# A two-stage strided convolution with a joint layer: first samples loaded in even and odd parts, taps issued by ScalarE, a leading tile of 396 columns

## The chip, the cores and the metric

The kernel runs on one core of a Trainium2 chip. The metric is the device time of one execution in microseconds, the median of several. The kernel before took 253.08 us, the median of three runs from 252.41 to 253.65.

The core's engines are named as in the profile: PE is TensorE (matrix products and transposes into PSUM), DVE is VectorE, ACT is ScalarE, POOL is GpSimd and SP is SyncE, which issues transfers here. Each engine works through its own list in order, and engines wait for each other by semaphores.

## The reference

Shapes: x is (2, 4000, 512), w1 and w2 are (5, 512, 512), g is (2, 8, 512), and w_f, w_g, w_o are (512, 512), all in bf16.

```python
xp = jnp.pad(x, ((0,0),(2,2),(0,0)))
h = sum over i of einsum("btc,cd->btd", xp[:, i:i+T, :], w1[i])
h = gelu(h)[:, ::2, :]                     # 2000 steps a sample
f = the same with w2 on h, gelu, [:, ::2]  # 1000 steps a sample
fe = f @ w_f ;  ge = g @ w_g
j = tanh(fe[:, :, None, :] + ge[:, None, :, :])
out = j @ w_o                              # (2, 1000, 8, 512)
```

So there are two convolutions of five taps, each with stride two, and then a joint layer over 16 pairs of sample and g row.

## The kernel before

Channels lie on the partitions, in four blocks of 128 (`NK`), and time steps are the columns of the matrix products. An output step t of the first convolution reads inputs 2t-2 to 2t+2.

The first convolution is done in two ways. A leading direct tile of the first sample makes `2 * NA` = 432 outputs, the plain way: five taps by four output blocks `m` by four input blocks `k`, 80 products of 432 columns (`direct`, lines 683 to 689), accumulated in PSUM banks 0 to 3. The taps go in the order 0, 4, 2, 1, 3. Taps 0, 4 and 2 read only even input steps, taps 1 and 3 only odd ones (`tap_at`, line 672). The rest goes through `Triple` (lines 554 to 596), which makes three outputs of a polyphase row together from nine products instead of fifteen. Its rows are sums and differences of six input phases (`z`, from xq or xp) that ACT and DVE make (`step`), and its weights are sums of taps that DVE and ACT make (`w1part`, lines 534 to 550: `ssum`, `w1_x` and `w1_t`). The first two triples are tiles of `N3` = 262 columns of the first sample, from `xq[0]` and `xq[1]`. Two triples for the second sample come from `xp[2]` and `xp[0]`, then two with w2 for the second convolution. Each triple is worked in four units, one for an output block, whose steps `s1` to `s5` interleave (lines 814 to 824).

The samples of the direct tile come as rows: `load_xr` (lines 445 to 449) puts four successive steps on one partition, 128 partitions in `xr[0]` and 90 in `xr[1]`. PE turns them with 32 transposes against `ident` (lines 493 to 508): for each of the two buffers, even steps (`pp` = 0), then odd ones. DVE copies the two results of `xr[0]` from PSUM to `xs[0]`, ACT those of `xr[1]`. Ahead of them PE runs eight products on zeros (`warm_mm`). The samples of the triples come by turning loads (`load_x6`, lines 451 to 456): a transfer that transposes, one for each of six phases, 272 columns each.

All loads of the head are issued by SP, in this order: `xr[0]`, `xr[1]`, w1[0] in two halves of its output columns, w1[4], w1[2], w1[1], w1[3], and then the turning loads of `xq[0]` (phases 4, 0, 2, 1, 3, 5), of `xq[1]` and of `xp[2]`. Each whole tap waits until the load three before it has landed (`o.after.append(came[-3].idx)`, line 469).

The order on each engine is planned by `Plan.schedule` (lines 157 to 225). It simulates the engines from the costs given with each operation, and for transfers from one shared wire: 1.8 us after issue a transfer may start, and it takes its bytes at a given rate (320 bytes a ns, 170 for turning loads). On PE, SP and POOL the lowest number among the ready operations goes first; on ACT and DVE the one that is due soonest. Up to `pl.pin = False` (line 694) the order of each engine is as written; from there on the plan sets it. At run time each engine follows the planned order strictly and waits for whatever comes late.

Of the kernel before, what the change touches and what calls it, by code (L numbers as in the profile page):

```python
# [50 lines left out]
class Psum:  # L51
# [6 lines left out]
    def pair(self, lo, step, n):  # L58
        ap = self.h[:, lo:lo + 2 * step].rearrange("p (s c) -> p s c", s=2)[:, :, 0:n]
        cells = np.unique(np.concatenate([np.arange(lo, lo + n), np.arange(lo + step, lo + step + n)]) // 512)  # L60
        return View(ap, cells, True)
# [6 lines left out]
class Plan:  # L68
# [25 lines left out]
    def dma(self, eng, fn, reads=(), writes=(), sem=None, nbytes=524288, rate=320e3):  # L94
# [3 lines left out]
        o.reads, o.writes, o.cost, o.pin, o.after, o.wire = tuple(reads), tuple(writes), 0.43, True, [], nbytes / rate  # L98
# [58 lines left out]
    def schedule(self, pred):  # L157
# [30 lines left out]
        wire, lock, start = 0.0, 0.0, [0.0] * n  # L188
        for _ in range(n):
# [24 lines left out]
            if o.dma:  # L214
                wire = max(wire, t + 1.8) + o.wire
                end = max(wire, t + 2.0)
# [85 lines left out]
def bass_standalone__seq2seq_rnn_t_joint__speech_kernel(  # L302
# [25 lines left out]
    NA, N3 = 216, 262  # L328
# [7 lines left out]
    NWARM = 8  # L336

    with ExitStack() as es:
# [106 lines left out]
        def load_xr(rt):  # L445
            n = NR[rt]
            dst = xr[rt].rows(0, n).map(lambda a: a.rearrange("p r k c -> p (r k c)"))
            src = x[0, 4 * P * rt:4 * (P * rt + n), :].rearrange("(p r) c -> p (r c)", r=4)
            return pl.dma("sp", lambda e: e.dma_start(dst.ap, src), (), (dst,), nbytes=n * 4 * 2 * D)

        def load_x6(buf, b, ph, j0, col, n=336):
# [4 lines left out]
            pl.dma("sp", lambda e: e.dma_start_transpose(out=dst.ap, in_=src), (), (dst,), nbytes=n * 2 * D, rate=170e3)  # L456

        came = [load_xr(rt) for rt in range(2)]
        act(warm[0:1], warm[1:2], ACT.Gelu_apprx_tanh)

        def load_w1(i):
            src = w1[i].rearrange("(k c) d -> c k d", c=P)
            if len(came) == 2:
                h = D // 2
                for sl in (slice(0, h), slice(h, D)):
                    o = pl.dma("sp", lambda e, sl=sl: e.dma_start(w1_sb[i, :, sl].ap, src[:, :, sl]), (), (w1_sb[i, :, sl],), nbytes=262144)
            else:
                o = load_w("sp", w1_sb[i], src)
                o.after.append(came[-3].idx)
            came.append(o)  # L470

        def load_xq(i, ph):
            load_x6(xq[i], 0, ph, 2 * NA // 3 + i * N3 - 2, 0, -(-(N3 + 3 - i) // 16) * 16)

        for kind, i in (('w', 0), ('w', 4), ('w', 2), ('w', 1), ('w', 3), ('x', 4), ('x', 0), ('x', 2), ('x', 1), ('x', 3), ('x', 5)):
            if kind == "w":
                load_w1(i)
            else:
                load_xq(0, i)
        for ph in (4, 0, 2, 1, 3, 5):  # L480
            load_xq(1, ph)
# [8 lines left out]

        warm_mm(NWARM)
        psb = ps.h[:, :].bitcast(BF16)
        for rt in range(2):
            for pp in range(2):
                bk, n = 4 + 2 * pp + rt, NR[rt]
                pv = View(psb[:, bk * 1024:(bk + 1) * 1024].rearrange("p (r k c) -> p r k c", r=2, k=NK)[:, :, :, 0:n], np.array([bk]), True)

                def fn(e, rt=rt, pp=pp, pv=pv, n=n):
                    for r in range(2):
                        for k in range(NK):  # L500
                            ins = e.transpose(pv.ap[:, r, k, :], xr[rt].h[0:n, 2 * r + pp, k, :], ident.h[0:n, 0:n])
                    return ins
# [184 lines left out]
        for i in taps:  # L687
            for m in range(NK):
                direct(i, m)
# [437 lines left out]
```

## Time and profile before

| what | value |
|---|---|
| median of three runs | 253.08 us (252.41 to 253.65) |
| profiled execution: its span | 251.3 us |
| profiled execution: own time beside the span | not listed on the page; the median is 1.8 us above the span |
| PE busy | 245.7 us, 98% |
| DVE, ACT busy | 211.8 us, 210.5 us |
| granted clock | 1.00 |
| first transpose, first product of the direct tile | 4.58 us, 7.47 us |
| first product of the first triple | 22.12 us |
| last landing of xr, w1, xq[0] | 5.86, 14.40, 24.27 us |

How to read it: times in the timeline are microseconds from the start of the span. The landing of a transfer is the last of its 16 semaphore updates in the trace. Products on PE are pipelined, so the listed length of one is longer than the distance to the next; where I give what a product costs, it is that distance. In the table by stage each engine has its busy time and its number of instructions. In the chain of waits each piece is what the next one waited for.

### The profile page before, as it was taken

The page shows a single profiled execution, that of the slowest core. Times are in us where ns is not written, and L with a number is a line of the kernel's source. Part 1 is how long each engine was busy: PE and PEld are TensorE (multiplying, and loading weights), DVE is VectorE, ACT ScalarE, POOL GpSimd, SP SyncE. Part 2 cuts the span into 40 slices and gives each one's busy share as a digit, 9 for nine tenths or more (in the row PEclk, how much of TensorE's full clock was granted, in tenths as well). Part 3 has the DMA queues.
Part 4 walks back from the last instruction along what each step waited for, and adds up shares of the span by engine and source line. Part 5 has one row for each costly group of instructions (what it writes and reads, how often), then busy time and mean ns, then how long its engine had stood idle before and what let it go on. Part 6 is the DMA issues. An engine that isn't in the chain of part 4 may idle for free.

```text
span 251.3 us, 5205 instructions
## 1 busy us (share of the span) xinstructions
PE 245.7 (98%) x1920; PEld 184.6 (73%) x1920; DVE 211.8 (84%) x347; ACT 210.5 (84%) x353; POOL 106.7 (42%) x109
## 2 busy tenths in 40 slices
PE   8999999999999999999999999999999999999994
PEld 4556788877666666666467878777788888778873
DVE  1699999967999997971547798999999999999892
ACT  2388699878959869963799999999999999997763
POOL 1000000000000000003338899698998999699930
PEclk9999999999999999999999999999999999999999
DMA  7999999988400052000002223322344336534648
GB/s 212 326 174 176 186 156 208 176 144 274 148 0 3 0 182 71 1 1 3 0 1 85 83 86 127 127 86 83 127 132 164 128 120 219 187 123 148 207 137 266
DMA packets 57392, 31.92 MB, mean 127 GB/s; under 512 B 33837, under 2 KB 57149, under 8 KB 57367
## 3 DMA queue, kind: packets, MB, share of 16 engines
q1 hardware_dynamic: 57367, 31.59, 48.0%
q8 instruction: 15, 0.25, 0.4%
q14 instruction: 10, 0.08, 0.1%
HBM read 7.71 MB, written 16.38 MB: 96 GB/s over the span
## 4 chain that ended last, share of the span: by engine, by line
PE 85%; DMA 6%; DVE 5%; ACT 2%; SPq 1%; issue 1%; DVEq 0%
PE acc L423 85%; DMA xq<-in_x_dram 3%; DMA w_sb<-in_w_dram 2%; DVE row L410 2%; DMA xr<-in_x_dram 1%; DVE xq L410 1%; SPq L456 1%; ACT sn L843 1%; DVE og L410 0%; ACT jT L415 0%; DVE sn L844 0%; DVE ssum L511 0%; ACT ost L843 0%; DVE w_t L410 0%; DVE w_x L410 0%
## 5 line engine op out<-in xcount | busy, mean ns | idle before, releaser
L410 DVE TENSOR_TENSOR og<-acc,sn 128x512 bf16<-128x512 f32 x87 | 56.9, 681 | 3.9 <-PE acc L423 3.1
L415 ACT ACTIVATE jT<-feT,geT 128x1000 bf16<-128x1000 f32 (+6 forms) x56 | 51.7, 975 | 0.5 <-DVE feT L736 0.4
L423 PE MATMUL acc<-tw,ss 128*128 128x256 f16 x348 | 48.0, 273 | 0.0
L912 POOL TENSOR_TENSOR ss<-jT 128x512 f16<-128x512 bf16 x28 | 33.8, 1219 | 12.9 <-ACT jT L415 10.6
L423 PEld LDWEIGHTS acc<-tw,ss 128*128 128x128 f16 x348 | 33.5, 98 | 7.3 <-DVE sn L844 0.3
L843 ACT ACTIVATE sn<-acc 128x512 f32<-128x512 f32 x52 | 31.5, 620 | 3.5 <-PE acc L423 3.2
L423 PE MATMUL acc<-row,w_sb 128*128 128x334 bf16 (+1 forms) x192 | 33.1, 295 | 0.2 <-DVE row L410 0.2
L423 PE MATMUL acc<-wo_sb,jT 128*128 128x256 bf16 (+1 forms) x196 | 31.7, 288 | 0.0
L407 POOL MEMSET hT<- 128x8 bf16 (+2 forms) x6 | 0.7, 148 | 71.8 <-ACT hT L415 66.8
L423 PE MATMUL acc<-row,w_x 128*128 128x262 bf16 (+1 forms) x192 | 28.2, 290 | 0.0
L415 ACT ACTIVATE jX<-feT,geT 128x1000 bf16<-128x1000 f32 (+4 forms) x28 | 25.0, 932 | 0.0
L423 PEld LDWEIGHTS acc<-row,w_sb 128*128 128x128 bf16 x192 | 18.5, 98 | 6.8 <-DVE row L410 0.5
L423 PEld LDWEIGHTS acc<-wo_sb,jT 128*128 128x128 bf16 x196 | 19.2, 98 | 5.3
L423 PEld LDWEIGHTS acc<-row,w_x 128*128 128x128 bf16 x192 | 18.8, 98 | 5.4
L415 ACT ACTIVATE sd<-acc 128x334 f32<-128x334 f32 (+1 forms) x48 | 20.5, 431 | 1.9 <-PE acc L423 1.3
L912 POOL TENSOR_TENSOR ss<-jX 128x512 f16<-128x512 bf16 x18 | 20.9, 1176 | 1.2 <-ACT jX L415 0.7
L415 ACT ACTIVATE hT<-acc 128x262 bf16<-128x262 f32 (+2 forms) x36 | 15.1, 432 | 6.7 <-PE acc L423 6.6
L511 DVE SCALAR_TENSOR_TENSOR acc<-acc,sd 128x334 f32<-128x334 f32 (+1 forms) x24 | 11.6, 483 | 10.4 <-PE acc L423 10.3
L844 DVE COPY sn<-acc 128x512 f32<-128x512 f32 x25 | 16.9, 682 | 2.4 <-PE acc L423 2.2
L423 PE MATMUL acc<-wo_sb,ss 128*128 128x256 bf16 x116 | 17.9, 273 | 0.0
L423 PE MATMUL acc<-hT,w_sb 128*128 128x334 bf16 x96 | 17.4, 305 | 0.0
L912 POOL TENSOR_TENSOR ss<-ss,jT 128x512 f16<-128x512 f16 x14 | 16.4, 1181 | 0.7 <-PE acc L423 0.4
(105 smaller groups left out, 501.6 us busy)
## 6 DMA issues: line engine op xcount, KB each, us to landing
out_dram<-og SPq DMA_DIRECT2D x44, 256.0 KB, 2.3
w_sb<-in_w_dram SPq DMA_DIRECT2D x9, 512.0 KB, 5.0
out_dram<-og SPq DMA_DIRECT2D x14, 128.0 KB, 2.7
out_dram<-ost SPq DMA_DIRECT2D x7, 128.0 KB, 2.0
xr<-in_x_dram SPq DMA_DIRECT2D x1, 512.0 KB, 3.4
w_sb<-in_w_dram SPq DMA_DIRECT2D x2, 256.0 KB, 5.1
wf_sb<-in_w_f_dram SPq DMA_DIRECT2D x1, 512.0 KB, 3.6
wg_sb<-in_w_g_dram SPq DMA_DIRECT2D x1, 512.0 KB, 4.7
```

The costliest lines, as they stand in the source:

```text
L407: pl.op("pool", lambda e: e.memset(v.ap, 0.0), (), (v,))
L410: pl.op(eng, lambda e: e.tensor_tensor(out=o.ap, in0=a.ap, in1=b.ap, op=op), (a, b), (o,), 0.02 + 2.14e-3 * o.ap.free_size() if eng == "po ...
L415: pl.op("act", lambda e: e.activation(o.ap, i.ap, func, scale=scale, bias=0.0 if bias is None else bias.ap), rd, (o,), o.ap.free_size() * ...
L423: ins = e.matmul(o.ap, lhsT=l.ap, rhs=r.ap, start=start and n == 0, stop=stop and n == len(pairs) - 1, skip_group_check=not check)
L456: pl.dma("sp", lambda e: e.dma_start_transpose(out=dst.ap, in_=src), (), (dst,), nbytes=n * 2 * D, rate=170e3)
L511: pl.op(eng, lambda e: e.scalar_tensor_tensor(out=o.ap, in0=a.ap, scalar=f, in1=b.ap, op0=ALU.mult, op1=add), (a, b), (o,), vec_cost(o, (a ...
L843: pl.flex({"act": (lambda e: e.activation(o.ap, v.ap, ACT.Copy), 0.05 + n * 0.833e-3), "dve": (lambda e: e.tensor_copy(out=o.ap, in_=v.ap) ...
L844: "dve": (lambda e: e.tensor_copy(out=o.ap, in_=v.ap), 0.065 + n * 1.04e-3)}, (v,), (o,))
L912: fn = lambda e, o=S[i], x=x, y=y, op=op: e.tensor_tensor(out=o.ap, in0=x.ap, in1=y.ap, op=op)
```

## The change

The change is confined to the head of the kernel, and to the sizes of the tiles of the first sample.

- `NA` goes from 216 to 198, so the direct tile has 396 columns; `N3` goes from 262 to 268; `xr[1]` has 72 partitions instead of 90.
- `load_xr` loads the even steps or the odd steps of a buffer, in runs of 1 KB. The even parts are issued by SP, the odd ones by ACT.
- The taps of w1 are issued by ACT, with no wait between them: w1[0] in two halves of its input blocks, w1[4], then the table load with the first activation, then the two odd parts of xr, then w1[2], w1[1], w1[3].
- SP issues the turning loads right behind the two even parts.
- PE: six products on zeros, the even transposes of `xr[0]`, two more on zeros, the even transposes of `xr[1]`, then tap 0 and tap 4, then the odd transposes of both, then taps 2, 1 and 3. DVE copies the even parts to `xs[0]`, ACT the odd ones.
- Tap 0 is done in halves: columns 0 to 127 of each group first, which need only `xr[0]`, then the other 70; and within each the input blocks 0 and 1 before 2 and 3.
- The memsets of the borders of `hT` are moved behind the taps.
- The planner has one wire for each issuing engine, 1.6 us from issue to start, other rates (245 for taps, 185 for turning loads, 80 for phases 4 and 0 of `xq[0]`), and the copies of the even parts cost 0.55 ns an element.

```diff
     def pair(self, lo, step, n):
-        ap = self.h[:, lo:lo + 2 * step].rearrange("p (s c) -> p s c", s=2)[:, :, 0:n]
+        lo_ap = self.h[:, lo:lo + n]
+        ap = bass.AP(tensor=lo_ap.tensor, offset=lo_ap.offset, ap=[list(lo_ap.ap[0]), [step, 2], [1, n]])
...
-        wire, lock, start = 0.0, 0.0, [0.0] * n
+        wire, lock, start = {}, 0.0, [0.0] * n
...
-                wire = max(wire, t + 1.8) + o.wire
-                end = max(wire, t + 2.0)
+                wire[e] = max(wire.get(e, 0.0), t + 1.6) + o.wire
+                end = max(wire[e], t + 2.0)
...
-    NA, N3 = 216, 262
+    NA, N3 = 198, 268
...
-    NWARM = 8
+    NWARM = 6
...
-        def load_xr(rt):
+        def load_xr(rt, pp, eng):
             n = NR[rt]
-            dst = xr[rt].rows(0, n).map(lambda a: a.rearrange("p r k c -> p (r k c)"))
-            src = x[0, 4 * P * rt:4 * (P * rt + n), :].rearrange("(p r) c -> p (r c)", r=4)
-            return pl.dma("sp", lambda e: e.dma_start(dst.ap, src), (), (dst,), nbytes=n * 4 * 2 * D)
+            dst = xr[rt].rows(0, n, slice(pp, 4, 2)).map(lambda a: a.rearrange("p r k c -> p r (k c)"))
+            src = x[0, 4 * P * rt:4 * (P * rt + n), :].rearrange("(p r) c -> p r c", r=4)[:, pp::2, :]
+            return pl.dma(eng, lambda e: e.dma_start(dst.ap, src), (), (dst,), nbytes=n * 2 * 2 * D)
...
-            pl.dma("sp", lambda e: e.dma_start_transpose(out=dst.ap, in_=src), (), (dst,), nbytes=n * 2 * D, rate=170e3)
-
-        came = [load_xr(rt) for rt in range(2)]
+            pl.dma("sp", lambda e: e.dma_start_transpose(out=dst.ap, in_=src), (), (dst,), nbytes=n * 2 * D, rate=rate, cost=n * 0.005)
+
+        def load_w1(i, parts=1):
+            n = NK // parts
+            for k in range(0, NK, n):
+                src = w1[i, k * P:(k + n) * P].rearrange("(k c) d -> c k d", c=P)
+                dst = w1_sb[i, k:k + n]
+                pl.dma("act", lambda e, dst=dst, src=src: e.dma_start(dst.ap, src), (), (dst,), nbytes=n * 131072, rate=245e3)
+
+        load_xr(0, 0, "sp")
+        load_w1(0, 2)
+        load_xr(1, 0, "sp")
+        load_w1(4)
         act(warm[0:1], warm[1:2], ACT.Gelu_apprx_tanh)
...
+        for rt in range(2):
+            load_xr(rt, 1, "act")
+        load_w1(2)
+        load_w1(1)
+        load_w1(3)
...
+        for i in range(2):
+            for ph in (4, 0, 2, 1, 3, 5):
+                load_xq(i, ph)
...
         warm_mm(NWARM)
...
+        turn(0, 0, "dve")
+        warm_mm(2)
+        turn(1, 0, "dve")
...
-        def both(i, k):
+        def both(i, k, q0=0, n=NA):
...
-        for i in taps:
+        for q0, n in ((0, P), (P, NA - P)):
+            for ks in ((0, 1), (2, 3)):
+                for m in range(NK):
+                    mm(ps.pair(m * NT + q0, NA, n), [(w1_sb[0, k, m * P:(m + 1) * P], both(0, k, q0, n)) for k in ks],
+                       q0 == 0 and ks[0] == 0, False, False)
+        for i in taps[1:]:
+            if i == 2:
+                turn(0, 1, "act")
+                turn(1, 1, "act")
             for m in range(NK):
                 direct(i, m)
+        for b in range(B):
+            memset(hT[b][4:6, :, HOFF - 1:HOFF])
+            memset(hT[b][:, :, HOFF + NT3:HOFF + NT3 + 2])
```

`turn(rt, pp, eng)` is the old body of the turning loop for one buffer and one parity, with the copy on the engine named.

## The prediction

> **What bounds the kernel now.** I read the page first (span and busy shares), then the table by stage, then the chain of waits, then the timeline of the first 34 us, and last the DMA view of three stretches.
>
> The page, span and the three busiest engines:
>
> ```profile
> span 251.3 us, 5205 instructions
> PE 245.7 (98%) x1920; PEld 184.6 (73%) x1920; DVE 211.8 (84%) x347; ACT 210.5 (84%) x353; POOL 106.7 (42%) x109
> ```
>
> PE is busy for 98% of the span, so time can only come off where PE is idle or where its columns become fewer. The same by stage (busy us of PE, PEld, DVE, ACT, POOL; clock; DMA share; GB/s):
>
> ```profile
> 1.20:7.47 6.27, 5.73 (x41) 3.34 (x41) 1.33 (x2) 1.85 (x4) 0.72 (x8) 1.00 0.97 273
> 7.47:22.12 14.65, 14.65 (x81) 7.84 (x81) 12.72 (x21) 9.95 (x15) 0.00 (x0) 1.00 1.06 226
> 22.12:28.83 6.71, 6.51 (x58) 5.31 (x56) 6.71 (x13) 5.75 (x13) 0.24 (x2) 1.00 1.03 185
> 28.83:60.00 31.17, 31.17 (x270) 26.31 (x271) 27.31 (x48) 26.14 (x51) 0.50 (x3) 1.00 1.02 180
> ```
>
> Up to 7.47 PE only warms up and turns samples; from 7.47 to 22.12 it runs the direct tile without a hole; from 28.83 on it is full again. Between 22.12 and 28.83 it has small holes while DVE is busy for all 6.71 us. So two things decide the head: when the direct tile can start, and whether DVE has the rows ready when it ends. The chain of waits says the second aloud (start, us, what):
>
> ```profile
> 0.74 3.43 DMA xr<-in_x_dram
> 4.19 4.75 DMA w_sb<-in_w_dram
> 11.51 6.42 DMA xq<-in_x_dram
> ...
> 28.17 0.61 DVE row L410
> 28.78 0.05 issue
> 28.83 185.64 PE acc L423 x1464
> ```
>
> PE is the end of the chain only from 28.83; before that it runs over transfers and DVE. And the timeline:
>
> ```profile
> 4.58 2.35 PE L501 MATMUL acc<-ident,xr 128*128 128x128 bf16 x32
> 7.47 14.81 PE L423 MATMUL acc<-xs,w_sb 128*128 128x432 bf16 x80 [0.54 <-ACT xs L415]
> 8.97 0.69 DVE L511 SCALAR_TENSOR_TENSOR ssum<-w_sb 128x512 f32<-128x512 bf16 x1 [1.96 <-DMA w_sb<-in_w_dram]
> 17.96 0.70 DVE L410 TENSOR_TENSOR row<-xq 128x1048 bf16<-128x1048 bf16 x1 [0.43 <-DMA xq<-in_x_dram]
> 28.83 0.62 PE L423 MATMUL acc<-row,w_sb 128*128 128x262 bf16 x4 [0.20 <-DVE row L410]
> ```
>
> DVE starts on the weight sums at 8.97, when w1[4] has landed, waits once (0.43 us, for phase 0 of xq), and has done 32 operations, one each 0.605 us, by 28.77. PE waits for the last of them. So DVE has no slack at 28.83.
>
> The landing records of the trace give: xr[0] 4.17, xr[1] 5.86, w1[0] 6.61 and 7.44, w1[4] 8.94, w1[2] 10.44, w1[1] 12.42, w1[3] 14.40, xq[0] phases 15.49, 17.94, 19.20, 20.93, 22.64, 24.27. The rates, from the DMA view of 2.5 to 4, 7 to 12 and 14 to 30 us:
>
> ```profile
> DMA packets 162, 0.60 MB, mean 399 GB/s; under 512 B 16, under 2 KB 16, under 8 KB 162
> DMA packets 1661, 1.65 MB, mean 331 GB/s; under 512 B 47, under 2 KB 1661, under 8 KB 1661
> DMA packets 11186, 2.80 MB, mean 175 GB/s; under 512 B 11185, under 2 KB 11185, under 8 KB 11185
> ```
>
> That is 4 KB packets of xr, 1 KB packets of w1, 256 B packets of the turning loads.
>
> **The change part by part.** The sum is made against this execution, span 251.3 us; the page gives no other time for it, the median of the runs is 253.08, so 1.8 us lies around the span and I add my difference to the median.
>
> *Start of the direct tile.* Tap 0 reads even phases only. It needs xr[0]'s even part (256 KB), which shares the engines with the first half of w1[0] on ScalarE's queue (256 KB): together the bytes that xr[0] had alone, so about 4.1 us (between 3.7, if SP's part goes first, and 4.4). Then PE does 8 transposes at 107 ns (the cold spacing from 4.58 to 5.86), two warm-up products at 0.427, and 8 transposes of 72 columns at 60 ns: 0.85 + 0.85 + 0.48, so tap 0 starts at 6.3, against 7.47. The DVE copy between (0.66, two in 1.33) ends at about 5.8, beside the warm-up products; the second one, 576 wide, is hidden under tap 0's first columns. xr[1]'s even part lands near 5.2, and w1[0]'s second half near 5.8, ahead of their use at 5.85 and 7.2. Going from 8 to 6+2 warm-up products costs nothing: they stand in time that PE has no data for. If w1[0] came only at 7.44 as before, this gain of 1.2 would be 0.3.
>
> *Direct tile.* 80 products of 432 columns took 14.65, or 183 ns each (180 of columns and 3). Now 396 columns: 64 at 168 ns and, tap 0 in halves, 16 of 256 and 16 of 140 columns, which sum to the same columns and 16 more times 3 ns: 13.5 us. The odd transposes, 16, move into it at full clock: 8 at 56 and 8 at 40 ns (the spacing of the 90-wide ones at the end of the old turning), 0.77. Their copies go to ScalarE (0.77 and some 0.6) under tap 2's 2.7 us; without that cover 1.4. End: 6.3 + 13.5 + 0.8 = 20.6, against 22.12: -1.5.
>
> *Two tiles of 268 for 262 columns.* 288 products x 6 / 2400 = +0.72 on PE, of which 0.58 after the first 56 products (those up to 28.83). DVE rows grow by 2%, some 0.16 by then. The loads stay 272 columns.
>
> *Queues.* Eight loads are issued by ScalarE at 0.4 to 0.5 each plus the 1.28 table load, about 5.5 us; its first work was at 6.64 and is now the odd copies near 10, so this is hidden. SP is past xr at 1.7 and issues turning loads at 1.31 to 1.57 each; the first went out at 9.37 before. The throttle on taps goes, so from then on both queues are in the engines together. This sets W, the landing of w1[2], from which DVE works on without a break: before it DVE has three operations of taps 0 and 4 alone (plus the first row operation if phases 4 and 0 are in). Ahead of W lie 2336 packets of 1 KB. Flow starts at 2.3 and landing follows the last packet by 0.8. Alone at 331 GB/s: 10.3. Taking turns packet by packet with 256 B ones (3.1 + 1.46 ns each at the rates above): 12.6. If the turning loads took half of the time: 15.1. If two queues hide each other's gaps and reach the 399 GB/s of the 4 KB row: 10.1. I take 11.0, between the two that are nearest to measured rows, on the early side because the 4 KB row shows that some of a 1 KB packet's time is not wire. W was 10.44, but DVE reached it in step then.
> The Trainium skill (DMA: Bandwidth & Descriptors, Issuing engines are not separate DMA queues) says that loads issued by several engines run on the same 16 DMA engines and interleave, and that this saves issue time alone; by it W would be the 12.6 and the result that of the slower rival below. Before only SP issued, so no row of before shows two queues at once; its rates fit one pool of engines.
>
> *DVE.* 3 operations by W, 29 more at 0.605: ready at W + 17.5 + 0.16 = 28.66 (28.06 with one row operation done in the gap), against 28.77. Two of the 32 (a row of the last step, si, and one weight sum) are used only after 29.3; if the planner's new order puts them later, 1.2 less.
> PE has run 56 products by 28.83; it could be there at 20.6 + 56 x 0.114 = 27.0.
>
> *Sum.* With DVE in its old order: 28.66 + 0.06 - 28.83 + 0.58 = +0.5. With PE free of all waits: -1.5 + 0.72 - 0.45 (the holes of 22 to 29) = -1.3. The gap operation (-0.6) and the freer order (-1.2) lie between, and their cover is the same 2 us that PE gains, so I take the middle: -0.4, 252.7 us: no change that can be told, since within 0.5% (1.27 us) is about what this kernel's measurements can't tell from none. After 60 us PE has no hole until 214, so the rest only shifts; a new order there may move some 0.3 either way.
>
> **The rivals.**
> 1. *Slower: the taps share the engines, and DVE is late.* Place: DVE between W and 29 us. Price: each us of W is a us at the end. From W = 11.8 on, with the old order, it is over 1.27 slower; at 12.6 it is 12.6 + 17.7 + 0.06 - 28.83 + 0.58 = +2.1, 255.1. It gets worse if DVE, in order, stands at the first row operation: the planner counts 80 GB/s for phases 4 and 0 and so has phase 0 at 10.5, where turns packet by packet give 15.5 (2176 packets of 4.55 ns after 4.8, and 0.8), up to +3.7. For it: DVE has no slack at 28.83, and it stood so at 17.96. Against it: xq comes far earlier than 15.49, and the order is planned anew.
> 2. *Faster: PE sets the end.* W near 10, phases 4 and 0 in by then, xr's even part at 3.7: tap 0 at 5.9, no holes: -1.3 - 0.4 = -1.7, 251.4. For it: before, PE's holes were only 0.45 in all. Against it: it asks for loads that don't feel each other.
> 3. *PE starves in the direct tile.* At half of the time w1[3] lands at 21.4 (2560 packets at 162 per us after 4.8) where tap 3 wants it at 17.9; direct ends at 24.1, and with W at 15.1 DVE is 4.5 late: about 257.5. For it only the fact that 256 B packets come in long trains; against it, a turning load's packets take a third of the time of a tap's (17 to 20 ns against 50).
>
> **How the numbers follow.** Forecast (no change, 252.7): 0.46, its own range 251.8 to 254.3. Faster: 0.24. Slower by DVE: 0.24. Starved: 0.06. So faster 0.24, same 0.46, slower 0.30. The range runs from 251.3, the faster rival, to 255.1, the slower one at 12.6; outside lie the starved case, the worse part of the slower one and a little below: 2 in 10.
> **What would show it.** Tap 0's first product at 5.9 to 6.6; the direct tile 14.2 to 14.4 long with the transposes in it; first row product at 20.3 to 21; w1[2] landing near 11 and phase 0 of xq under 12; PE's holes from there to 30 us 0.3 to 1.5 in all. The forecast is wrong if DVE stands for over 1 us at w1[2] or at a row while PE waits, if w1[1] or w1[3] hold PE in the direct tile, or if the holes vanish altogether.

## The result and the profile after

The changed kernel took 260.47 us (median of four runs, 259.48 to 262.89) beside 252.75 us for the kernel before on the same chip: a ratio of 1.031 with a 95% interval from 1.026 to 1.037. It is slower by 7.7 us, where 252.7 us had been forecast. One run of the experiments below (261.84 us, of `f1_told`) fell in a slower state of the chip and is left out of its ratio. The profiled execution took 259.48 us; its last product on PE starts at 254.51 us, against 247.77 us before.

The page of the changed kernel, span, engines and clock by slice:

```profile
span 257.7 us, 5250 instructions
...
PE 246.9 (96%) x1932; PEld 186.3 (72%) x1936; DVE 211.5 (82%) x347; ACT 209.9 (81%) x353; POOL 106.5 (41%) x109
...
PEclk9589999999999999999999999999999999999999
```

PE is busy 1.2 us longer than before although it has less to do in the direct tile, and DVE and ACT are busy as long as before. So most of the loss is waiting. The clock row shows a stretch at half clock in the second and third slice (6.4 us each). The same stretches as in the table by stage shown of before (busy us of PE, PEld, DVE, ACT, POOL; clock; DMA share; GB/s):

```profile
1.20:7.47 6.27, 3.78 (x16) 1.26 (x16) 0.69 (x1) 1.49 (x2) 0.44 (x4) 1.00 0.84 261
7.47:22.12 14.65, 12.56 (x92) 8.85 (x93) 6.67 (x12) 4.82 (x6) 0.00 (x0) 0.77 1.18 225
22.12:28.83 6.71, 5.87 (x38) 3.44 (x36) 6.71 (x12) 6.31 (x10) 0.24 (x2) 1.00 1.12 194
28.83:60.00 31.17, 30.49 (x266) 25.96 (x267) 31.17 (x55) 27.11 (x55) 0.53 (x6) 1.00 0.94 152
```

In the second row DVE does 6.67 us of work where it did 12.72, and ACT 4.82 where it did 9.95. What they left undone there is what PE lacks later. The timeline of PE, with two lines of ACT (start, length, what, in brackets the idle time before and what ended it):

```profile
5.30 0.59 PE L424 MATMUL acc<-zero 128*128 128x512 bf16 x2
8.73 0.66 PE L501 MATMUL acc<-ident,xr 72*128 72x72 bf16 x8 [2.84 <-DMA xr<-in_x_dram]
9.20 8.12 PE L424 MATMUL acc<-xs,w_sb 128*128 128x256 bf16 x48
...
13.59 1.10 ACT L416 ACTIVATE row<-xq 128x1080 bf16<-128x1080 bf16 x1 [9.84 <-DMA xq<-in_x_dram]
...
18.40 1.10 ACT L416 ACTIVATE row<-xq 128x1080 bf16<-128x1080 bf16 x1 [3.71 <-DMA xq<-in_x_dram]
...
19.93 1.54 ACT L416 ACTIVATE xs<-acc 128x1024 bf16<-128x1024 bf16 x2
...
21.53 5.55 PE L424 MATMUL acc<-xs,w_sb 128*128 128x396 bf16 x32 [0.82 <-ACT xs L416]
...
26.91 1.08 PE L424 MATMUL acc<-row,w_x 128*128 128x268 bf16 x8
...
29.51 2.00 PE L424 MATMUL acc<-row,w_x 128*128 128x268 bf16 x16 [1.51 <-ACT sd L416]
```

PE waits for `xr[1]`'s even part, starts tap 0 at 9.20 at half clock, waits for the odd copies on ACT ahead of tap 1, and waits again at 29.51. The odd copies (19.93) had their input at 17.8, but ACT works in order and stood at two rows that wait for turning loads. The waits say the same (total us, times, longest):

```profile
ACT row L416 <- DMA xq<-in_x_dram: 13.6, 2, 9.8
...
DVE ssum L516 <- DMA w_sb<-in_w_dram: 3.2, 1, 3.2
DVE row L411 <- DMA xq<-in_x_dram: 2.8, 1, 2.8
```

And the chain of waits (start, us, what):

```profile
4.29 14.09 DMA xq<-in_x_dram
...
18.40 0.72 DVE row L411
...
28.18 0.98 ACT xq L416
29.17 0.29 ACT sd L416
...
29.51 106.49 PE acc L424 x802
```

Phase 0 of `xq[0]` is 14.09 us under way, then DVE, and from 27.16 on ACT, have work without a longer gap until PE is full at 29.51. The landings, from the trace's semaphore records, with four kernels of the experiments below:

```
landing, us     before   after  e5_held  k1_queues  p4_whole  q1_pe_only
xr[0] (even)      4.17    4.79     4.73       4.36      4.31        4.34
xr[1] (even)      5.86    8.68     7.96       6.61      6.62        5.78
w1[0], 2nd half   7.44    5.46     5.50       7.24      7.17        7.02
w1[4]             8.94    8.18     8.80       9.05      8.89       10.12
xr[0], xr[1] odd     -   9.72,12.48 9.84,10.65   -         -           -
w1[2]            10.44   14.84    12.02      10.99     10.75       11.62
w1[3]            14.40   18.51    14.80      14.84     14.64       14.60
xq[0] phase 4    15.49   13.56    15.78      11.39     11.21       15.52
xq[0] phase 0    17.94   18.38    17.26      15.06     14.85       17.95
first turning load issued
                  9.37    2.53    12.03       1.69      1.66       10.54
```

The turning loads go out 6.8 us earlier than before, but phase 0 lands 0.4 us later, and every tap from w1[2] on 4.1 to 4.4 us later.

On PE the loss of 6.74 us adds up as follows: start of tap 0 +1.73 (9.20 against 7.47); half clock +2.5 (16 products at 213 ns and 16 at 117, where `h1_sp` below has 110 and 62); hole ahead of tap 1 +0.99; odd transposes +0.71; 80 products of 36 columns less -1.15; hole behind the first row products 1.68, before 0.45 in all: +1.23; larger triples +0.72. That is 6.7. It says where PE stood, not yet why.

### The profile page after: what moved, and what is told of

It is laid out like the page before. It is cut to its first block, busy times and chain, and to the rows that moved or that the text cites. A ratio compares the mean times of both kernels' runs of the same rounds, so it can differ in the third digit from the quotient of the medians.

```text
span 257.7 us, 5250 instructions
## 1 busy us (share of the span) xinstructions
PE 246.9 (96%) x1932; PEld 186.3 (72%) x1936; DVE 211.5 (82%) x347; ACT 209.9 (81%) x353; POOL 106.5 (41%) x109
## 4 chain that ended last, share of the span: by engine, by line
PE 85%; DMA 5%; DVE 4%; ACT 2%; SPq 1%; issue 1%; DVEq 0%
PE acc L424 85%; DMA xq<-in_x_dram 5%; DVE row L411 2%; ACT sn L856 1%; SPq L457 1%; SPq L450 1%; DVE ssum L411 1%; DVE xq L411 0%; DVE og L411 0%; ACT xq L416 0%; ACT jT L416 0%; DVE sn L857 0%; DVE w_t L411 0%; ACT ost L856 0%; DVE ssum L516 0%
## 5 line engine op out<-in xcount | busy, mean ns | idle before, releaser
L925 POOL TENSOR_TENSOR ss<-jT 128x512 f16<-128x512 bf16 x28 | 33.8, 1220 | 12.9 <-ACT jT L416 10.1
L424 PE MATMUL acc<-row,w_x 128*128 128x268 bf16 (+1 forms) x192 | 29.3, 291 | 1.5 <-ACT sd L416 1.5
L416 ACT ACTIVATE hT<-acc 128x268 bf16<-128x268 f32 (+2 forms) x36 | 15.3, 429 | 6.4 <-PE acc L424 6.1
L416 ACT ACTIVATE row<-xq 128x1080 bf16<-128x1080 bf16 x6 | 6.5, 1099 | 13.9 <-DMA xq<-in_x_dram 13.6
```

The lines of the kernel that those rows point to most:

```text
L416: pl.op("act", lambda e: e.activation(o.ap, i.ap, func, scale=scale, bias=0.0 if bias is None else bias.ap), rd, (o,), o.ap.free_size() * ...
L424: ins = e.matmul(o.ap, lhsT=l.ap, rhs=r.ap, start=start and n == 0, stop=stop and n == len(pairs) - 1, skip_group_check=not check)
L925: fn = lambda e, o=S[i], x=x, y=y, op=op: e.tensor_tensor(out=o.ap, in0=x.ap, in1=y.ap, op=op)
```

## The experiments

Each ratio is against the kernel before on the same chip, with its 95% interval. Diffs are against the changed kernel (after) unless another is named. Theory A, the first: PE starts late and loses its clock, and that is the loss. Theory B: the loads land late because the split samples and the turning loads are in the engines together, and ACT and DVE, in an order that counts on them early, stand at them.

**Is it the late start and the clock?** Three ways to give PE an earlier start or a full clock, with the loads' order kept. `e4_bridge` puts eight instead of two products on zeros between the even transposes:

```diff
         turn(0, 0, "dve")
-        warm_mm(2)
+        warm_mm(8)
         turn(1, 0, "dve")
```

> Eight products on zeros instead of two stand between the even transposes of xr[0] and those of xr[1]; nothing else differs. In the changed kernel PE stood 3.0 us there (5.51 to 8.73) for xr[1]'s even part, the granted clock was 0.5 from 7.61 to 14.43, and tap 0 ran at half rate. Theory A (late even part and the clock it costs): tap 0 still starts near 9.2, but at full rate, so it ends near 11.9 instead of 14.35 and the whole is up to 2.6 us shorter, about 258. Theory B (ScalarE and VectorE stand in order behind the turning loads, so PE only waits later): tap 2 ends 2.6 us earlier, but tap 1 still starts near 21.5 because ScalarE copies the odd parts only after phase 0 of xq at 18.4; the time stays within 0.5 of 260.5.

Measured: 264.95 us, 1.0497 [1.0450, 1.0544]. The clock was full from 9.86 to 23.51 and tap 0 ran at full rate, and the kernel was 1.8% slower than after. Timeline of `e4_bridge`:

```profile
25.84 7.74 PE L424 MATMUL acc<-xs,w_sb 128*128 128x396 bf16 x32 [7.24 <-ACT xs L416]
```

Its waits (total us, times, longest):

```profile
ACT row L416 <- DMA xq<-in_x_dram: 14.9, 2, 9.8
PE acc L424 <- ACT xs L416: 7.2, 1, 7.2
```

PE comes to tap 1 earlier, and waits 7.24 us for the same odd copies on ACT. The clock falls there. `e1_late_turn` moves the even transposes of `xr[1]` behind tap 0's first columns:

```diff
         warm_mm(2)
-        turn(1, 0, "dve")
...
         for q0, n in ((0, P), (P, NA - P)):
+            if q0:
+                turn(1, 0, "dve")
```

> The even transposes of xr[1] are moved on PE behind tap 0's first 128 columns, which do not need them; the loads are the same. Theory A: tap 0 starts near 6.2 at full clock, its second part near 9.4, tap 2 ends near 17, and the whole is 3 to 4 us shorter, about 257. Theory B: tap 1 still starts near 21.5, PE then stands 3 to 4 us before it, and the time stays within 0.7 of 260.5.

Measured: 262.85 us, 1.0415 [1.0369, 1.0462]. Tap 0 started at 7.11, tap 2 ended at 17.8, tap 1 began at 23.68. Every one of these kernels is planned anew: here and in `e4_bridge` ACT has three rows of `xq` ahead of the odd copies (they ran at 22.08 and 24.24), in after two (19.93). So part of what `e1_late_turn` and `e4_bridge` lose against after is their order and not the earlier PE. `e3_rows80` loads the parts of `xr[1]` with 80 partitions instead of 72 (the trace shows 12 of the 16 engines' updates for 72):

```diff
-            n = NR[rt]
+            n = -(-NR[rt] // 16) * 16
```

> xr[1]'s parts are loaded with 80 partitions instead of 72 (the last 8 are not used), which 16 divides; the rest is the changed kernel. Its landing records with 72 showed 12 updates that come with data, with 90 before 15. If the odd number of partitions makes these parts late, the even part lands near 5.5 to 6 instead of 8.7, and the odd one near 10.5 instead of 12.5. If lateness is the queue of loads issued before it, it lands at 8 or later. The whole stays within 1 us of 260.5 either way, since ScalarE holds tap 1.

Measured: 260.93 us, 1.0310 [1.0256, 1.0364]: no change from after. The even part did land at 7.10 (8.68), tap 0 started at 7.42 at full clock and the first row product came at 24.50, 2.4 us earlier than in after; then PE stood 4.6 us. Timeline of `e3_rows80`:

```profile
30.00 3.50 PE L424 MATMUL acc<-row,w_x 128*128 128x268 bf16 x16 [4.42 <-ACT sd L416]
```

The chain ahead of this wait goes back over ACT and DVE to a turning load (phase 2) that landed at 20.91. So theory A is not the cause by itself: in all three an earlier PE waits longer at the next place. The times of after itself say so too: its profiled run has a mean clock of 0.985, the other three 0.993, and those took longer (260.2 to 262.9 us).

`e2_xr1_first` issues `xr[1]`'s even part from ScalarE ahead of the taps:

```diff
         load_xr(0, 0, "sp")
+        load_xr(1, 0, "act")
         load_w1(0, 2)
-        load_xr(1, 0, "sp")
```

> xr[1]'s even part is issued by ScalarE ahead of the taps instead of by SP behind xr[0]'s. If loads are served about in the order of issue whatever the queue, it lands near 4.5 to 5.5 instead of 8.7 and tap 0 starts near 6.3 at full clock. Theory A: 3 to 4 us shorter, about 257. Theory B: tap 1 still starts near 21.5 and the time stays within 0.7 of 260.5. If the 72 partitions themselves make the load late, it lands after 7 here too and nothing changes.

Measured: 261.19 us, 1.0348 [1.0278, 1.0418]. It landed at 5.52, but w1[0] then came at 8.48 and 9.25 and w1[2] at 17.86: the wait went to another load.

**Is it the turning loads beside the others?** `e5_held` makes SP wait with the turning loads until w1[2] has landed:

```diff
         load_w1(2)
+        w2nd = pl.ops[-1].idx
...
                 load_xq(i, ph)
+                if i == 0 and ph == 4:
+                    pl.ops[-1].after.append(w2nd)
```

> The first turning load waits on SP until w1[2] has landed; the rest is the changed kernel. Theory B (turning loads that run beside the taps delay both): w1[2] lands near 10 to 11 instead of 14.84, w1[3] near 14, phase 0 of xq near 17 or later, VectorE gets to its weight sums 4 us earlier, and the whole is 1.5 to 3 us shorter, 257.5 to 259, although tap 0 still starts near 9.2. Theory A: no gain but what the taps' arrival gives in the direct tile, which is none, since PE never stood for a tap: within 0.7 of 260.5.

Measured: 259.69 us, 1.0280 [1.0246, 1.0314]. The table of landings holds the main finding: the first turning load is issued 9.5 us later than in after, and yet w1[2] lands 2.8 us earlier, w1[3] 3.7 and phase 0 1.1; only phase 4 is later, by 2.2, and the last phase of `xq[0]` comes at 23.70 instead of 24.08. The DMA view of after, 8 to 11 us:

```profile
DMA packets 994, 0.48 MB, mean 159 GB/s; under 512 B 697, under 2 KB 994, under 8 KB 994
```

The same of `e5_held`:

```profile
DMA packets 863, 0.85 MB, mean 284 GB/s; under 512 B 31, under 2 KB 863, under 8 KB 863
```

The same of before:

```profile
DMA packets 1017, 1.01 MB, mean 337 GB/s; under 512 B 31, under 2 KB 1017, under 8 KB 1017
```

In after, the engines move less than half of what they moved before. SP shows it as well: the first four turning loads took 1.71, 4.67, 5.22 and 3.65 us to issue (1.3 to 2.8 before). But PE stayed late in `e5_held` (tap 0 at 8.47, half clock until 14.01), so the total hardly moved, as theory A expects. The edit changes the planned order too: the odd copies on ACT ran at 17.21, before any row of `xq`. `f2_held_late` is `e5_held` with the late turn of `e1_late_turn` (against `e5_held`):

```diff
         warm_mm(2)
-        turn(1, 0, "dve")
...
+            if q0:
+                turn(1, 0, "dve")
```

> Two edits together: turning loads wait for w1[2], and the even transposes of xr[1] stand behind tap 0's first columns. Each alone gave 259.7 and 262.9. With the turning loads held the planner put the odd copies ahead of the rows (17.21 there), so what the late transposes give PE is no longer lost to ScalarE. Theory A plus B: tap 0 starts near 6.5 to 7, no long half-rate stretch, the direct tile ends near 21 to 22 instead of 25.3; VectorE, with w1[2] at 12.0, is ready at 12.0 + 17.7 = 29.7 and then sets the end, 1 to 2 us above the kernel before: 254 to 255. If VectorE's time from w1[2] on is not what sets the end, it is 252 or less, or unchanged near 259.7.

Measured: 255.31 us, 1.0115 [1.0074, 1.0156]. Of the 3.1% two thirds are gone. The same late turn that cost 1% with the loads of after gains 1.65% here. The table by stage of `f2_held_late`:

```profile
7.47:22.12 14.65, 12.79 (x96) 7.94 (x95) 12.34 (x21) 8.52 (x12) 0.00 (x0) 0.88 1.13 237
22.12:28.83 6.71, 6.71 (x54) 5.12 (x53) 6.71 (x12) 6.03 (x13) 0.24 (x2) 1.00 0.96 183
```

DVE is back at 12.34 us of work, and PE has no hole in the second row. What is left lies before 22 us: PE waits 1.0 us for `xr[1]` and 1.2 us for DVE's copy of it, which stands in order behind two weight sums that wait for w1[4] (landed at 8.55), and the clock is half from 10.94 to 14.35. So it takes both: earlier loads for ACT and DVE, and an earlier PE.

`f3_w2_ahead` is `f2_held_late` with w1[2] issued ahead of the odd parts; `g1_held_late_80` is it with 80 partitions; `g2_held_first` is `e5_held` with the order of `e2_xr1_first`. In this order:

```diff
-        for rt in range(2):
-            load_xr(rt, 1, "act")
         load_w1(2)
         w2nd = pl.ops[-1].idx
+        for rt in range(2):
+            load_xr(rt, 1, "act")
```

```diff
-            n = NR[rt]
+            n = -(-NR[rt] // 16) * 16
```

```diff
+        load_xr(1, 0, "act")
         load_w1(0, 2)
-        load_xr(1, 0, "sp")
```

> As the run before it, with w1[2] issued ahead of the two odd parts of xr instead of behind them. These 400 KB take 1.2 us at 331 GB/s, so w1[2] lands near 10.8 and the odd parts near 12. Theory: VectorE's end moves with w1[2] one for one, so 1.0 to 1.2 us less than the run before it, 253 to 254. If PE or the rows of xq set the end, no difference over 0.5.

> Turning loads held until w1[2] has landed, the even transposes of xr[1] behind tap 0's first columns, and xr[1]'s parts loaded with 80 partitions (with 80 alone the even part landed at 7.10 instead of 8.7). Against 255.3 for the first two together: the waits of 1.0 and 1.19 in the direct tile and the half-rate stretch of 1.3 us go or shrink, tap 0 starts near 6, the direct tile ends near 21 to 22. If PE's start still sets the end, 2 to 3 us less, 252.5 to 253.5. If VectorE sets it, with its last row for the first unit near 30, no more than 1 less, 254.3 to 255.5.

> Turning loads held until w1[2] has landed, and xr[1]'s even part issued by ScalarE ahead of the taps; the order on PE is that of the changed kernel. If w1[0] came late in the run with that part first (8.48 and 9.25) because a turning load had been issued ahead of it, it lands near 6 to 7.5 here, tap 0 starts near 6.5 to 7.5 at full clock, and the time is near that of the run with 80 partitions, 253 to 255. If the slow issue of 72 partitions (1.45 us on ScalarE) is what delays w1[0], it lands near 8 again and the time stays at 256 or more.

Measured, in this order: 256.00 us, 1.0145 [1.0099, 1.0190]; 254.85 us, 1.0082 [1.0051, 1.0113]; 255.82 us, 1.0113 [1.0062, 1.0164]. None of the three can be told from `f2_held_late`. In `f3_w2_ahead` w1[2] came at 10.36 instead of 11.95 and PE's first row product at 22.81, and nothing was gained: PE stood 0.85 us for a row of DVE at 25.02, which DVE began only 0.64 us earlier than in `f2_held_late` (24.16 against 24.80), and again for DVE at 72.15. So "each us of W is a us at the end" did not hold there. Why DVE gained so little is open; its order is another one here too. In `g1_held_late_80` the part of `xr[1]` was in at 6.91, and PE still stood 2.09 us for DVE's copy of it, again behind the two sums that wait for w1[4]. In `g2_held_first` the first row product came at 22.65, near before's 22.12, with two waits for taps on the way.

**Is it the planned order?** `f1_told` leaves the loads of after and gives the planner rates that reproduce their measured landings, so that it orders ACT and DVE for them. `p2_queues_told` does the same for `k1_queues` below.

Of `f1_told`:

```diff
+            rate = {(0, 0): 107e3, (1, 0): 37.8e3, (0, 1): 175e3, (1, 1): 54.6e3}[rt, pp]
...
-                    80e3 if i == 0 and ph in (4, 0) else 185e3)
+                    {4: 58e3, 0: 58e3, 2: 348e3, 1: 113e3}.get(ph, 185e3) if i == 0 else 185e3)
```

> The changed kernel with the planner alone told the landing times that its trace showed (phase 4 of xq at 13.5, phase 0 at 18.4, w1[2] at 14.8 and so on). Loads, sizes and the order up to the taps are the same. Theory B1 (the planner took the turning loads for 6 to 8 us earlier than they come, so ScalarE has two rows of xq planned ahead of the odd copies and VectorE a row ahead of the weight sums): the odd copies run near 17.5 to 19, PE's hole before tap 1 (0.99) goes, the hole of 1.68 at 27.7 shrinks, and the whole is 1 to 2.5 us shorter, 258 to 259.5. Theory B2 (the late taps and rows themselves set VectorE's end): the hole before tap 1 goes, but the first full stretch of products still starts near 29, so within 0.7 of 260.5.

Measured: 258.16 us (255.87 to 258.68), 1.0172 [1.0104, 1.0241]. The odd copies ran at 18.02 and the hole ahead of tap 1 was gone, although the loads landed later still in its profiled run (phase 0 at 19.77). The order alone is worth some 1.4% of the 3.1%; its interval and that of after nearly touch, so the size is rough.

**Which part of the change costs what?** `k1_queues` is the kernel before with only the queues and the planner's times of the change: samples whole, 432 columns, old turning (against before):

```diff
...
-        came = [load_xr(rt) for rt in range(2)]
...
+        load_xr(0)
+        load_w1(0, 2)
+        load_xr(1)
+        load_w1(4)
...
+        load_w1(2)
+        load_w1(1)
+        load_w1(3)
...
+        for i in range(2):
+            for ph in (4, 0, 2, 1, 3, 5):
+                load_xq(i, ph)
```

`p2_queues_told` (against `k1_queues`; the rates of `xr` and of the taps are told in the same way):

```diff
...
-                    80e3 if i == 0 and ph in (4, 0) else 185e3)
+                    {4: 58e3, 0: 76e3, 2: 410e3, 1: 113e3, 3: 380e3, 5: 209e3}[ph] if i == 0 else 185e3)
```

`h1_sp` keeps the split samples and PE's part, with all loads on SP, the old planner rates, and the wait of whole taps for the load three before:

```diff
...
+                if parts == 1:
+                    o.after.append(came[-3].idx)
...
+        came = [load_xr(rt, 0, "sp") for rt in range(2)]
...
         load_w1(0, 2)
         for rt in range(2):
-            load_xr(rt, 1, "act")
+            load_xr(rt, 1, "sp")
+        load_w1(4)
```

`p4_whole` loads whole samples by SP and keeps the rest of the change:

```diff
...
-            src = x[0, 4 * P * rt:4 * (P * rt + n), :].rearrange("(p r) c -> p r c", r=4)[:, pp::2, :]
+            src = x[0, 4 * P * rt:4 * (P * rt + n), :].rearrange("(p r) c -> p (r c)", r=4)
...
-        for rt in range(2):
-            load_xr(rt, 1, "act")
```

`q1_pe_only` keeps only PE's part (transposes in two groups, tap 0 in halves, 396 columns): whole samples, all loads on SP, the old rates (against `p4_whole`); `q2_pe_216` is that with the old tile sizes.

```diff
...
+                if parts == 1:
+                    o.after.append(came[-3].idx)
...
+        came = [load_xr(rt, 0, "sp") for rt in range(2)]
...
         load_w1(0, 2)
```

```diff
-    NA, N3 = 198, 268
+    NA, N3 = 216, 262
```

> The kernel before with the queues alone changed: taps issued by ScalarE with no wait between them, turning loads on SP right behind xr, and the planner's new wires and rates. xr is loaded whole, the direct tile has 432 columns and tap 0 is whole. Theory: w1[2] lands near 13 to 15 instead of 10.44, phase 4 and phase 0 of xq near 13 and 18, VectorE waits for both in order, and the time is 3 to 5 us above the kernel before, 256 to 258; tap 0 starts near 7.5 at full clock and the direct tile ends near 22.5, since its copies stand ahead of the rows on ScalarE. If the early turning loads were worth what they were to bring, it would be 252 or less.

> The changed kernel with its loads put back on SP in the order of the kernel before (even parts, w1[0] in two halves, odd parts, the other taps each waiting for the load three before it, then the turning loads), and the planner's wire as before. Even and odd parts, tap 0 in halves and 396 columns stay. Theory (the two queues together make the loss): w1[2] lands near 10.5 to 11 and phase 0 of xq near 18, the odd copies are not held, tap 0 starts near 6.5 to 7 and the time is within 1.2 of the kernel before, 252 to 254. If the halves, the parts or the smaller tile cost by themselves, it is 255 or more.

> The changed kernel with xr loaded whole by SP, in runs of 4 KB as before, and nothing in place of the odd parts on ScalarE; two queues, order on PE, halves of tap 0 and 396 columns stay. If the split of xr is what slows the loads, w1[2] lands near 11 and phase 0 of xq near 15, as with the queues alone on the kernel before; the odd copies run some 3 us earlier, and the time falls from 260.5 to 255 to 257. If the two queues do it whatever the split, w1[2] lands after 13.5 and the time stays above 258.

> Edit: every load and its order is that of before (all on SP, xr whole, each whole tap behind the load three before it, one wire in the planner with its old rates); of the change only PE's part is kept: even transposes first, odd ones between taps 4 and 2, tap 0 in halves, 396 columns in the direct tile and 268 in the two triples. Theory (the loads were the whole loss): tap 0 near 6.8 at full clock, direct tile 13.5 + 0.8 long, so first row product near 21.2 against 22.12; VectorE's rows and sums come when they did before, so a hole of about 1 us stands where 0.45 stood, and the end is before + 0.72 - 0.5 or so: 252.2 to 253.8, within 0.5% of before. Rival (halves, the later odd transposes or the smaller tile cost something by themselves): 254.2 or more, with a hole before tap 1 on PE or a VectorE that is later than 28.8 with the last row.

> Edit: as q1_pe_only, but with the tile sizes of before (432 columns in the direct tile, 262 in the triples). Theory (columns moved into the triples cost 0.72 while VectorE sets the time of the first row products anyway): 0.3 to 0.7 us faster than q1_pe_only, 251.6 to 253.2; the direct tile ends near 22.0 and the hole behind it is under 0.6. Rival (PE's start decides and the smaller tile pays): not faster than q1_pe_only.

> The kernel before with the queues alone changed, and the planner told the landing times that the trace of that kernel showed. If the order made for wrong times is what its holes come from (0.65 and 0.66 between 23 and 25, 0.80 at 54.9), they go and it comes from 255.5 to 253 to 254; if the late w1[2] (11.0 against 10.44) and the later start (8.0 against 7.5) make it, no more than 0.7 is gained.

Measured, as ratios to before:

```
                                    one queue (SP)             two queues, turning loads early
samples whole, before's PE           1                          k1_queues       1.0108 [1.0060, 1.0156]
  the same, planner told                                        p2_queues_told  1.0069 [1.0052, 1.0085]
samples whole, the change's PE       q1_pe_only 1.0040 [1.0020, 1.0060]   p4_whole  1.0140 [1.0108, 1.0172]
  with 432 columns                   q2_pe_216  1.0033 [1.0011, 1.0055]
samples split, the change's PE       h1_sp      1.0113 [1.0068, 1.0158]   after     1.0313 [1.0256, 1.0370]
```

So the split costs 0.7% on one queue (`h1_sp` less `q1_pe_only`) and 1.7% on two (after less `p4_whole`); two queues cost 1.0% with whole samples and 2.0% with split ones. Added up, split and queues alone make 1.7%; together they cost 2.7%. The excess of 1.0%, 2.5 us, is known to about 0.8% either way by the four ratios, and `h1_sp` is not quite after on one queue (its odd parts stand ahead of w1[4], and taps wait for earlier loads), so its size is rough. `k1_queues` missed what was expected of it: w1[2] landed at 10.99 and not at 13 to 15, so two queues by themselves hardly delay the taps. Telling its planner the landings (`p2_queues_told`) made a difference of 0.4%, which the two intervals do not tell from none. The excess is seen in the engines too. The DMA view of 8 to 11 us of `k1_queues`, turning loads beside taps without split samples:

```profile
DMA packets 1733, 1.07 MB, mean 356 GB/s; under 512 B 899, under 2 KB 1733, under 8 KB 1733
q10 hardware_dynamic: 865, 0.85, 84.1%
```

The same of after has this row for ScalarE's queue (packets, MB, share of 16 engines' time):

```profile
q10 hardware_dynamic: 312, 0.30, 51.2%
```

That is 356 GB/s with both kinds in turn (865 packets of ScalarE's queue, 868 of SP's); the parts of samples beside taps alone made 284; all three together 159. The engines are not idle in after, but each packet takes about twice as long: 79 ns on ScalarE's queue (0.512 x 16 x 3 us over 312) against 47 in `k1_queues`, and on SP's 39 against 18. The 72 partitions are not the main reason: with 80 (`e3_rows80`) all three kinds together made 208 GB/s in the same stretch, still far under 284 and 356. `h1_sp` has its own loss: w1[4] landed at 11.78 behind the odd parts. Timeline of `h1_sp`:

```profile
5.58 2.93 PE L424 MATMUL acc<-xs,w_sb 128*128 128x256 bf16 x32
11.82 4.29 PE L424 MATMUL acc<-xs,w_sb 128*128 128x396 bf16 x16 [3.32 <-DMA w_sb<-in_w_dram]
```

Tap 0 did start at 5.58, as early as the change can make it, and the gain was lost at the next tap. `p1_sp_80` is `h1_sp` with the 80 partitions of `e3_rows80`. `p3_odd_sp` is after with them, the late turn, and the odd parts on SP ahead of the turning loads. Their lines:

```diff
-            n = NR[rt]
+            n = -(-NR[rt] // 16) * 16
```

```diff
         for rt in range(2):
-            load_xr(rt, 1, "act")
+            load_xr(rt, 1, "sp")
```

> All loads on SP in the order of before, with xr[1]'s parts of 80 partitions instead of 72. With 72, w1[4] landed at 11.78 and PE stood 3.5 us for it, and from 12 to 13.5 the engines moved 50 to 80 GB/s, as if a few had all the work. If the 72 partitions do that, w1[4] lands near 9 to 9.5, PE's wait falls under 1 us, full clock stays, and the time falls from 255.5 to 252.5 to 253.5. If the 1 KB runs do it, w1[4] stays after 11 and the time at 255.

> The changed kernel with the odd parts issued by SP ahead of the turning loads instead of by ScalarE among the taps, with 80 partitions, and with the even transposes of xr[1] behind tap 0's first columns. If odd parts beside turning loads are what slows both, the engines move about 360 GB/s from 7 us on, w1[2] lands near 11 to 11.5, phase 0 of xq near 15 to 16, and the time falls to 254 to 256. If not, w1[2] lands after 13.5 again and the time stays above 257.

Measured: 255.23 us, 1.0102 [1.0077, 1.0127], with w1[4] at 10.99 still; so 72 partitions are not the main cause there. And, for `p3_odd_sp`, 258.84 us, 1.0245 [1.0230, 1.0260]: the engines moved 285 GB/s from 8 to 11 us instead of 159 and w1[2] landed at 12.02, as theory B has it, but phase 0 still landed at 16.42, PE waited 2.2 us ahead of tap 1, and the time missed what was expected.

`q1_pe_only` shows PE's part by itself, 253.96 us against 253.09. Its timeline:

```profile
6.48 2.91 PE L424 MATMUL acc<-xs,w_sb 128*128 128x256 bf16 x32 [0.18 <-issue]
10.16 2.87 PE L424 MATMUL acc<-xs,w_sb 128*128 128x396 bf16 x16 [0.78 <-DMA w_sb<-in_w_dram]
...
24.36 2.44 PE L424 MATMUL acc<-row,w_x 128*128 128x268 bf16 x20 [1.09 <-DVE row L411]
```

Tap 0 starts 1.0 us earlier than before; 0.78 of it goes in the wait for w1[4] and 1.09 in the wait for DVE. Part of both is the kernel's own making: as w1[0]'s halves count as two loads in it, w1[4] waits for `xr[1]` where it waited for `xr[0]` before, and it and w1[2] land 1.2 us later (10.12 and 11.62), which its expectation had not seen. So what PE's part is worth with before's own waits stays open; the 0.4% holds with these later taps. Taking the smaller tile out (`q2_pe_216`) made no difference that can be told. No version run is faster than the kernel before.

## Why the prediction was wrong, step by step

*The limits were read rightly.* "DVE has no slack at 28.83", and "two things decide the head: when the direct tile can start, and whether DVE has the rows ready when it ends". `e3_rows80` bears it out: its first row product came 2.4 us earlier than in after, PE then stood 4.6 us at the end of a chain over DVE, and nothing was gained. `e4_bridge` shows a third limit that the prediction did not ask for: ACT.

*The step that failed: when the loads land, and DVE without a break behind them.* W was put at 11.0 and phase 0 of `xq[0]` under 12, and W was the landing "from which DVE works on without a break". W was 14.84 and phase 0 landed at 18.38; DVE stood 3.24 us at w1[2] and 2.78 at phase 0. This is the step that carries most of the loss: with the turning loads held and the late turn (`f2_held_late`) two thirds of it are gone, and with whole samples and nothing else of the loads changed (`p4_whole`: w1[2] at 10.75, phase 0 at 14.85) more than half.

*Start of the direct tile: the first to fail in time.* `xr[1]`'s even part was put "near 5.2", without bounds; it landed at 8.68, behind w1[0] and w1[4] and not beside them (at 7.10 with 80 partitions, at 5.52 issued ahead of the taps). As its transposes stand ahead of tap 0 on PE, tap 0 came at 9.20, not 6.3. `xr[0]`'s part came at 4.79, above the bounds given (3.7 to 4.4). The clock was not in the sum at all: the 2.84 us without products brought half clock for 6.83 us, +2.5. Winning it back alone gained nothing (`e3_rows80`); with the loads held, the late turn was worth 1.65%.

*Direct tile.* 13.5 + 0.8 was expected; from 9.20 to 26.91 it took 17.7: 14.2 by its columns and transposes, 2.5 for the clock, 1.0 for the hole. The odd copies were costed at nothing under tap 2, and 1.4 without that cover. The cover was ACT's freedom, and ACT stood at rows of xq. What is queued ahead of the copies on their own engine was not asked.

*W.* 11.0 was taken between 10.1 and 15.1; it was 14.84. `k1_queues` (10.99) and `p4_whole` (10.75) show that 11.0 was right for two queues with whole samples: the packets of taps and turning loads took turns, at 356 GB/s, better than either alone. The odd parts are among the 2336 packets of the sum, but at the rate of taps alone; what it left out is that all three kinds together move 159 GB/s. The Trainium skill (DMA: Bandwidth & Descriptors, Issuing engines are not separate DMA queues) says that such loads interleave on the same engines. The turns in `k1_queues` agree. The 12.6 of the prediction took each packet at the time that it has alone, and neither 10.99 nor 14.84 is near it. For phase 0 the same working, 15.5 in rival 1, is near what `k1_queues` showed (15.06), and the "under 12" was wrong even without split samples.

*Queues.* Turning loads were to take 1.31 to 1.57 us each on SP; they took up to 5.22 while taps were in the engines, so going out 6.8 us earlier bought phase 4 1.9 us and phase 0 nothing.

*DVE.* With the measured W the prediction's formula gives 14.84 + 17.66 + 0.06 = 32.56 for the first product with `row` and `w_sb`, which came at 33.17. That they are near is luck. The formula has no stand at phase 0; the new order put other operations in between; and PE did not wait there: DVE's last row before it was done by 32.03, and PE had been full since 29.51. What PE waited for last is `sd` of ACT at 29.51, and the chain ahead of it starts at phase 0. Rival 1 (slower, DVE late, and worse "if DVE, in order, stands at the first row operation") named this mechanism and the place: DVE stood 2.78 us there. Its chance and the range, which ended at 255.1, were too small: the range stopped at W = 12.6 and left the stand at phase 0 outside. Rival 3 had the nearest time, 257.5, by another cause: PE never waited for a tap here.

*Larger triples* cost the 0.72 that the sum says by their columns; `q2_pe_216` against `q1_pe_only` shows no difference in the whole that can be told.

## What to carry to other kernels

A load that is issued earlier is not a load that lands earlier: in `e5_held`, holding the first of the turning loads back by 9.5 us brought the taps from w1[2] on in 2.8 to 3.7 us sooner and the last phase of the first tile 0.4. Give every landing that an in-order engine waits for its own bounds, and ask what stands ahead of each moved instruction on its engine, not only what it could hide under. Where PE and DVE both arrive just in time, moving one alone is worth nothing, and may cost the clock.

## What the runs showed of the hardware

- Rates depend on the mix. From 8 to 11 us: taps with split samples 284 GB/s (`e5_held`), taps with turning loads 356 (`k1_queues`), all three 159 (after). In the last each packet takes about twice as long as in `k1_queues`. Which step of a transfer makes it slow is open; the trace shows only the packets.
- The granted clock changes in steps of 3.41 us (half from 7.61 to 14.43 in after, two steps). The Trainium skill (TensorE: Matmul & The Clock Gate, Part 1: The HAM clock gate) names a free-running window of 3413 ns; the trace agrees. The Trainium skill (the same page, Why this matters for your kernels) warns of idle gaps of over about 3 us. Here less was enough, and what counted was PE's idle time within one step: 2.09 us in `g1_held_late_80`, 2.15 in `p1_sp_80`, and two holes of 1.0 and 1.2 in `f2_held_late` were each followed by a step at half clock; 1.92 in `e3_rows80` and 2.05 in `p3_odd_sp` (of a hole of 2.20 that lay across the end of a step) were not.
- A part of 72 partitions brought the updates of 12 engines and landed at 8.68 (after); with 80 partitions it landed at 7.10 (`e3_rows80`). The Trainium skill (DMA: Bandwidth & Descriptors, Why a DMA increments its semaphore by 16 and not by 1) says that the number of engines must divide the access pattern's slowest dimension; 72 and 12 agree with it.
